# Keys and values in one ring of three 32 KB rows, and probabilities spread by 32 transposes a group, copied out by two engines

## The chip, the cores and the metric

The kernel runs on one NeuronCore of a Trainium2 chip. The metric is device time in microseconds (us) of one execution. The core has five engines that run their own instruction streams: TensorE (PE, matrix multiply, with its weight loads shown as PEld), VectorE (DVE), ScalarE (ACT), GpSimd (POOL) and SyncE (SP), which here only issues DMA transfers. Each stream is in order; an instruction waits on semaphores for what other engines or transfers must have finished. Everything behind a waiting instruction in the same stream waits too.

## What is computed

One decode step (one token, batch 1) of an attention block followed by a small MLP block. Cut to what matters here:

```python
# A: attention with a key/value cache; 32 query heads share 8 key/value heads, 4 to each
q = layernorm(x) @ wq                       # [1, 512] @ [512, 32*128]
scores = einsum("bhqd,bhkd->bhqk", q, k) * 128 ** -0.5     # k_cache [1, 8, 16384, 128] bf16
p = softmax(scores)
o = einsum("bhqk,bhkd->bhqd", p, v)         # v_cache [1, 8, 16384, 128] bf16
h = x + o.reshape(1, 1, 32 * 128) @ wo      # wo [4096, 512]
# B: with one token the shifted mixer gives zero, so hs @ w2 adds nothing; what is left is
y = layernorm(h)
out = h + y + gelu(layernorm(y) @ w3) @ w4  # w3 [512, 1792], w4 [1792, 512]
```

The bytes are almost all cache: 8 heads of keys and 8 of values, 4 MB (4,194,304 bytes) each, 67 MB in all. With wq and wo (4 MB each) and w3 and w4 (1.8 MB each) it is 79.2 MB.

## The kernel before

**Groups.** One key/value head with its four query heads is a group g, 0 to 7. A head's 16384 tokens lie as 128 partitions of 128 consecutive tokens, so one load of keys is 128 rows of 32 KB, one row to a partition.

**Buffers.** Keys have two buffers of 32 KB a partition (`kb`, L200). Values come in two halves of 8192 tokens, each 128 rows of 16 KB, into three buffers of 16 KB a partition (`vb`, L202); the two halves of the last group go into `kb[0]`. Together 112 KB a partition. The weights w3 and w4 go into `kb[1]` at the end.

**One round** of the loop at L461, for g from 0 to 8, does the scores of group g and the value sums of group g-1:

- DVE transposes the keys in 32x32 blocks, eight instructions a group (L379), from `kb` into `kt`. After the fourth of them the first half of the scores can be finished, after the eighth the second half.
- PE makes the scores in two halves of 16 matmuls each (L388) in `s_ps`: 128 partitions (column tile, query head) by 512 tokens a half.
- DVE takes the maximum of each half (L396); two small PE steps with DVE steps between them (L401 to L410) make one bias per head.
- ACT takes the exponential of each half (L414) into `p_sb`, 128 by 1024, and POOL copies its first 64 columns behind its end (L420).
- `weights(g)` (L422) brings the probabilities to the layout that the value sums need, tokens on partitions. PE transposes 16 windows of 128 columns, each 64 columns further than the last (L424), into the PSUM tile `T_ps`, which fills two banks, windows 0 to 7 and 8 to 15. DVE copies what is wanted out of them into `pt` with five copies of 64 partitions (L430).
- `denominator(g)` (L435) adds up the exponentials with two small matmuls.
- `values(g-1, A, qs)` (L444) multiplies `pt` of the group before with the value half A, 16 matmuls a half, into `O_ps`. In the order of PE the 16 of half A=0 stand between the two halves of the scores, the 16 of A=1 in two eights around the small steps of the maximum.
- `gather(g-1)` (L453, L456): DVE copies `O_ps` to `o_sb`, and PE adds it into `A_ps` with eight matmuls in fp32. In PE's order it stands behind `weights(g)`, and in DVE's order behind the copies of L430.

Round 8 has only values(7) and gather(7). Behind it come the division by the denominators, the product with wo (128 matmuls, L522), the second block's layernorm (a chain of small DVE instructions, L254 to L295), the products with w3 (L535) and w4 (L555) and the output.

**The queue of loads.** All loads of the loop are issued by SP at the end of each round, in order: x4 (by ACT), wq, k0, k1, then values of g (two halves) and keys of g+2 for each g, and after those of g=7 wo in three pieces, w3 in two, w4 in two. Each issue waits until the buffer that it fills has been read: a key load until the eight transposes of the group two before are done, a value load until the value matmuls of the buffer's last user are done.

**Order by hand.** `Program.op` (L35) works out the waits from the keys that an operation reads and writes, and from the PSUM banks it uses (an operation waits for the last one of every other engine on its bank). Operations of one engine keep the order in which they are written.

Of the kernel before, what the change touches and what calls it, by code (L numbers as in the profile page):

```python
# [112 lines left out]
HKV = 8  # L113
SK = 16384
DH = 128
# [8 lines left out]
KRING = 2  # L124
VRING = 3
VT = 64 * DH
# [4 lines left out]
def bass_sequential_preLN__gqa_block_cached__mixer_s_mlp__decode_kernel(  # L131
# [13 lines left out]
    with ExitStack() as ctx:  # L145
# [3 lines left out]

# [33 lines left out]
        p_sb = sb("p_sb", [128, 1024 + 64], BF16)  # L183
        pt = [sb(f"pt{i}", [128, 4, 2, 16, REP], BF16) for i in range(2)]
# [15 lines left out]
        kb = [sb(f"kb{i}", [128, 128 * DH], BF16) for i in range(KRING)]  # L200
        kt = sb("kt", [128, 128 * DH], BF16)
        vb = [sb(f"vb{i}", [128, VT], BF16) for i in range(VRING)]  # L202
        w3_sb = kb[1][:, 0:NCH * FM].rearrange("p (k f) -> p k f", k=NCH)
        w4_sb = kb[1][:, NCH * FM:2 * NCH * FM].rearrange("p (m c) -> p m c", m=NHC)
# [12 lines left out]
        def load_k(g):  # L217
            i = g % KRING
            load(f"k{i}", kb[i][:, :], A_k_cache[0, g].rearrange("(p t) d -> p (t d)", p=128), ("k", i, 0),
                 also=[("k", i, n) for n in range(1, 4)])  # L220

        def value_tile(g, A):

            if g == HKV - 1:
                return kb[0][:, A * VT:(A + 1) * VT], ("k", 0, A)
            i = (2 * g + A) % VRING
            return vb[i][:, :], ("v", i)

        def load_v(g, A):
            src = A_v_cache[0, g, A * 8192:(A + 1) * 8192, :].rearrange("(p t) d -> p (t d)", p=128)  # L230
            dst, key = value_tile(g, A)
            load("v" + "_".join(map(str, key[1:])), dst, src, key)
# [69 lines left out]
        load_k(0)  # L302
        load_k(1)
# [70 lines left out]
        def transpose_keys(g, ts):  # L374
            i = g % KRING
            for t in ts:
                view = lambda x, t=t: x[:, :].bitcast(I32).rearrange("p (x l w) -> p x (l w)", x=2, l=64)[
                    :, :, t * 512:(t + 1) * 512]
                dve(lambda e, i=i, view=view: e.transpose(view(kt), view(kb[i])),  # L379
                    r=[("k", i, n) for n in range(4)], w=[("kt", t)])  # L380

        ktv = kt[:, :].rearrange("p (x l b s e) -> p b e l x s", x=2, l=64, b=2, s=32, e=2)

        def scores(g, half):
            for n in range(4):
                for ct in range(4):
# [4 lines left out]
                        ktv[:, n // 2, n % 2, 8 * c8:8 * c8 + 8, :, :],  # L391
# [15 lines left out]
        def max_c(g):  # L407
# [5 lines left out]
            for half in range(2):  # L413
                act(lambda e, half=half, g=g: e.activation(  # L414
                    p_sb[:, half * 512:half * 512 + 512].rearrange("p (l s x) -> p l x s", l=8, x=2),
                    s_ps[:, half, :].rearrange("p (l x s) -> p l x s", l=8, x=2),
                    ACTF.Exp, bias=bias[:, 0:1], scale=float(SCALE), accum_out=acc[g % 2][:, half:half + 1]),
                    r=[("s", half), "bias"], w=[("p", half), ("acc", g % 2)], bank=[("s", half)])
                if half == 0:
                    P.op("POOL", lambda e: e.tensor_copy(p_sb[:, 1024:1088], p_sb[:, 0:64]), r=[("p", 0)], w=[("p", 2)])  # L420

        def weights(g):  # L422
            for w in range(16):
                pe(lambda e, w=w: e.transpose(T_ps[:, w, :], p_sb[:, w * 64:w * 64 + 128], ident[:, :]),  # L424
                   r=[("p", w // 8), ("p", (w + 1) // 8), "ident"], w=[("T", w // 8)], bank=[("T", w // 8)])
            to = pt[g % 2][:, :, :, :, :].rearrange("p c A l h -> p l (c A) h")
            of = T_ps[:, :, :].rearrange("p w (k o u h) -> p w k o u h", o=2, u=2, h=REP)
            for half, lo, w0, w1, l0 in ((0, 0, 0, 8, 0), (0, 64, 0, 8, 1), (1, 0, 8, 16, 8), (1, 64, 8, 15, 9),
                                         (1, 64, 15, 16, 0)):
                dve(lambda e, lo=lo, w0=w0, w1=w1, l0=l0: e.tensor_copy(  # L430
                    to[lo:lo + 64, l0:l0 + w1 - w0, :, :], of[lo:lo + 64, w0:w1, :, lo // 64, 0, :]),
                    r=[("T", half)], w=[("pt", g % 2)], bank=[("T", half)])
# [6 lines left out]
        def values(g, A, qs):  # L439
            tile, key = value_tile(g, A)  # L440
            for q in qs:
                for ct in range(4):
                    n = 32 * (q // 2) + 8 * ct + 4 * (q % 2)
                    pe(lambda e, q=q, ct=ct, n=n: e.matmul(  # L444
                        O_ps[g % 2][32 * ct:32 * ct + 16, :],
                        pt[g % 2][:, ct, A, 4 * q:4 * q + 4, :].rearrange("p l h -> p (l h)"),
                        tile[:, n * DH:(n + 4) * DH],
                        start=(A == 0 and q == 0), stop=(A == 1 and q == 3)),
                       r=[key, ("pt", g % 2)], w=[("O", g % 2)], bank=[("O", g % 2)])
# [11 lines left out]
        for g in range(HKV + 1):  # L461
# [6 lines left out]
            if g:  # L468
                values(g - 1, 0, range(4))
# [5 lines left out]
            if g:  # L475
                values(g - 1, 1, range(2))
            if g < HKV:
                max_b()
            if g:
                values(g - 1, 1, range(2, 4))  # L480
# [9 lines left out]
            if g < HKV:  # L490
                for A in range(2):
                    load_v(g, A)
                if g + 2 < HKV:
                    load_k(g + 2)
            if g == HKV - 1:
# [4 lines left out]
                for n, (lo, hi) in enumerate(W3):  # L500
                    load(f"w3{n}", w3_sb[:, lo:hi, :], w3_in[:, lo:hi, :], ("k", 1, n))
                w4_in = B_w4.rearrange("(p m) c -> p m c", p=128)
                for n, (lo, hi) in enumerate(W4):
                    load(f"w4{n}", w4_sb[:, lo:hi, :], w4_in[:, lo:hi, :], ("k", 1, 2 + n))
# [90 lines left out]
```

## Time and profile before

| | |
|---|---|
| median of 3 runs | 194.05 us (194.0 to 194.56) |
| the profiled execution | 194.11 us, of which the span from first to last instruction is 192.3 us |
| busy over the span | PE 112.5 us (58%), DVE 122.0 us (63%), ACT 16.9 us (9%), POOL 3.3 us (2%) |
| moved by DMA | 79.32 MB, mean 412 GB/s over the span |
| key transposes (L379) | 64 in 74.0 us, mean 1212 ns |
| transposes of probabilities (L424) | 128 in 11.7 us, mean 249 ns each while they overlap |
| copies out of them (L430) | 40 in 9.8 us |
| exponentials (L414) | 16, mean 822 ns |
| granted TensorE clock | mean 0.761 of full; in each part either 1.0 or 0.5 |

Lines of the profile name the source line, the engine, the operation, output and input tiles, and shapes. In a timeline row the first number is the start in us from the begin of the span, the second the length of the merged stretch; `x7` is the number of instructions in it, and the bracket is the time that the engine sat idle before it, with what ended that idle time. SPq is SP's instruction stream, in which a DMA row is the issue of a transfer, not the transfer.

### The profile page before, as it was taken

To read this page: it belongs to the slowest core of one execution; us is meant where nothing else is said; L and a number is where in the kernel's file an instruction comes from. 1 tells how busy PE (TensorE), PEld (TensorE's weight loads), DVE (VectorE), ACT (ScalarE), POOL (GpSimd) and SP (SyncE) were. 2 spreads that over 40 slices of the span, in tenths; PEclk is the share of its full clock that TensorE was granted. 3 is DMA by queue.
4 is the path that set the end of the run, shared out by engine and by line. 5 is a ranking of instruction groups with operands and counts; after the bars stand their busy time and mean duration, and the time that the engine had idled before them with its cause. 6 is when DMAs were issued, how large, how long until landed. Compare 5 with 4: busy or idle time off the path is not lost.

```text
span 192.3 us, 2624 instructions
## 1 busy us (share of the span) xinstructions
PE 112.5 (58%) x1106; PEld 56.3 (29%) x1106; DVE 122.0 (63%) x236; ACT 16.9 (9%) x38; POOL 3.3 (2%) x17
## 2 busy tenths in 40 slices
PE   1025046567837766774776558645885676594533
PEld 1025001242234235223422522242223422453402
DVE  5834099499449928964894379536944796403274
ACT  3000000030030030003000200030003000600010
POOL 2000000000000000000000000000000000000000
PEclk9999999999985695588559655975558559669555
DMA  6999999999999999999999999999999999999990
GB/s 225 429 436 433 436 436 426 423 455 436 395 429 467 436 388 429 460 423 409 426 436 436 419 423 436 443 426 416 450 441 399 416 429 436 417 421 424 421 376 34
DMA packets 4634, 79.32 MB, mean 412 GB/s; under 512 B 528, under 2 KB 528, under 8 KB 912
## 3 DMA queue, kind: packets, MB, share of 16 engines
q1 hardware_dynamic: 4616, 79.17, 96.8%
q8 instruction: 8, 0.13, 0.3%
q14 instruction: 2, 0.02, 0.0%
q10 hardware_dynamic: 8, 0.00, 0.0%
HBM read 79.17 MB, written 0.00 MB: 412 GB/s over the span
## 4 chain that ended last, share of the span: by engine, by line
DMA 47%; DVE 18%; issue 2%; PE 2%; SPq 1%; ACT 0%; DVEq 0%; ACTq 0%
DMA kb<-in_A_k_cache_dram 28%; DMA wqo<-in_A_wo_dram 19%; DVE kt L379 13%; PE O_ps L522 1%; DVE mx L396 1%; DVE st L293 1%; SPq L215 1%; DVE hcol L546 1%; DVE sti L295 0%; PE T_ps L424 0%; DVE pt L430 0%; PE mn_ps L260 0%; ACT hg L542 0%; DVE xs L550 0%; DVE st L295 0%
## 5 line engine op out<-in xcount | busy, mean ns | idle before, releaser
L379 DVE STREAM_TRANSPOSE kt<-kb 128x1024 int32<-128x1024 int32 x64 | 74.0, 1212 | 11.1 <-DMA kb<-in_A_k_cache_dram 11.0
L388 PE MATMUL s_ps<-kt,qb 128*32 128x512 bf16 x256 | 47.7, 557 | 32.0 <-DVE kt L379 32.0
L444 PE MATMUL O_ps<-vb,pt 128*16 128x512 bf16 x224 | 29.2, 533 | 0.0
L388 PEld LDWEIGHTS s_ps<-kt,qb 128*32 128x32 bf16 x256 | 10.7, 114 | 61.6 <-DVE kt L379 53.9
L414 ACT ACTIVATE p_sb<-s_ps,bias 128x512 bf16<-128x512 f32 x16 | 12.7, 822 | 149.9 <-PE mn_ps L408 113.8
L456 PE MATMUL A_ps<-o_sb,zo 128*128 128x128 f32 x64 | 15.7, 422 | 10.5 <-DVE o_sb L453 10.5
L430 DVE COPY pt<-T_ps 64x256 bf16<-64x256 bf16 (+2 forms) x40 | 9.8, 261 | 15.5 <-PE T_ps L424 15.2
L396 DVE TENSOR_REDUCE mx<-s_ps 128x1 f32<-128x512 f32 x16 | 10.8, 677 | 11.9 <-PE s_ps L388 9.8
L424 PE MATMUL T_ps<-ident,p_sb 128*128 128x128 bf16 x128 | 11.7, 249 | 11.0 <-ACT p_sb L414 11.0
L456 PEld LDWEIGHTS A_ps<-o_sb,zo 128*128 128x128 f32 x64 | 13.4, 311 | 11.6 <-DVE o_sb L453 11.6
L424 PEld LDWEIGHTS T_ps<-ident,p_sb 128*128 128x128 bf16 x128 | 8.8, 111 | 12.9 <-ACT p_sb L414 12.7
L444 PEld LDWEIGHTS O_ps<-vb,pt 128*16 128x16 bf16 x224 | 9.4, 115 | 10.0 <-issue 8.5
L357 PE MATMUL mn_ps<-xn,wqo 128*128 128x1 bf16 x128 | 3.6, 165 | 9.4 <-DMA wqo<-in_A_wq_dram 9.4
L401 PE MATMUL mn_ps<-ident_f,mx 128*1 128x128 f32 x32 | 7.3, 322 | 2.5 <-DVE mx L396 2.5
L453 DVE COPY o_sb<-O_ps 128x512 f32<-128x512 f32 x8 | 5.5, 692 | 5.0 <-PE O_ps L444 4.7
L357 PEld LDWEIGHTS mn_ps<-xn,wqo 128*128 128x128 bf16 x128 | 3.5, 104 | 9.4 <-issue 9.4
L404 DVE TENSOR_REDUCE nm<-mn_ps 1x4 f32<-1x256 f32 x8 | 3.3, 406 | 3.7 <-PE mn_ps L401 3.7
L522 PE MATMUL O_ps<-wqo,o_b 128*32 128x128 bf16 x128 | 3.1, 271 | 2.9 <-DMA wqo<-in_A_wo_dram 1.6
L420 POOL COPY p_sb<-p_sb 128x64 bf16<-128x64 bf16 x8 | 1.9, 237 | 160.5 <-ACT p_sb L414 160.5
L401 PEld LDWEIGHTS mn_ps<-ident_f,mx 128*1 128x1 f32 x32 | 2.3, 90 | 7.5 <-DVE mx L396 5.3
L408 PEld LDWEIGHTS mn_ps<-nm,nscale 1*128 1x128 f32 x16 | 2.5, 198 | 5.5 <-DVE nm L404 5.5
L408 PE MATMUL mn_ps<-nm,nscale 1*128 1x4 f32 x16 | 3.2, 270 | 1.2 <-DVE nm L404 0.9
(75 smaller groups left out, 51.7 us busy)
## 6 DMA issues: line engine op xcount, KB each, us to landing
kb<-in_A_k_cache_dram SPq DMA_DIRECT2D x8, 4096.0 KB, 26.3
vb<-in_A_v_cache_dram SPq DMA_DIRECT2D x14, 2048.0 KB, 24.2
wqo<-in_A_wq_dram SPq DMA_DIRECT2D x1, 4096.0 KB, 12.3
kb<-in_A_v_cache_dram SPq DMA_DIRECT2D x2, 2048.0 KB, 26.8
wqo<-in_A_wo_dram SPq DMA_DIRECT2D x2, 1792.0 KB, 34.7
kb<-in_B_w_dram SPq DMA_DIRECT2D x1, 1344.0 KB, 22.9
kb<-in_B_w_dram SPq DMA_DIRECT2D x1, 1280.0 KB, 26.2
wqo<-in_A_wo_dram SPq DMA_DIRECT2D x1, 512.0 KB, 37.4
```

What stands on the lines that cost most here:

```text
L357: pe(lambda e, h=h, k=k: e.matmul(n_ps[:, h:h + 1], wqo[:, k * HQ * DH + h * DH:k * HQ * DH + (h + 1) * DH], xn[:, k:k + 1], start=(k == 0 ...
L379: dve(lambda e, i=i, view=view: e.transpose(view(kt), view(kb[i])), r=[("k", i, n) for n in range(4)], w=[("kt", t)])
L388: pe(lambda e, g=g, half=half, n=n, ct=ct, c8=c8: e.matmul(s_ps[32 * ct:32 * ct + 32, half, :], qb[:, n, g, :, :, :].rearrange("p a u h -> ...
L396: dve(lambda e: e.tensor_reduce(mx[:, half:half + 1], s_ps[:, half, :], AX.X, ALU.max), r=[("s", half)], w=[("mx", half)], bank=[("s", half)])
L401: pe(lambda e, half=half: e.matmul(m_ps[0:1, half * 128:half * 128 + 128], mx[:, half:half + 1], ident_f[:, :], start=True, stop=True), r= ...
L408: pe(lambda e: e.matmul(n_ps[:, 0:REP], nscale[0:1, :], nm[0:1, :], start=True, stop=True), r=["nm", "nscale"], w=["n"], bank=["mn"])
L414: act(lambda e, half=half, g=g: e.activation(p_sb[:, half * 512:half * 512 + 512].rearrange("p (l s x) -> p l x s", l=8, x=2), s_ps[:, hal ...
L424: pe(lambda e, w=w: e.transpose(T_ps[:, w, :], p_sb[:, w * 64:w * 64 + 128], ident[:, :]), r=[("p", w // 8), ("p", (w + 1) // 8), "ident"] ...
L430: dve(lambda e, lo=lo, w0=w0, w1=w1, l0=l0: e.tensor_copy(to[lo:lo + 64, l0:l0 + w1 - w0, :, :], of[lo:lo + 64, w0:w1, :, lo // 64, 0, :]) ...
L444: pe(lambda e, q=q, ct=ct, n=n: e.matmul(O_ps[g % 2][32 * ct:32 * ct + 16, :], pt[g % 2][:, ct, A, 4 * q:4 * q + 4, :].rearrange("p l h -> ...
L453: dve(lambda e, g=g: e.tensor_copy(o_sb[g % 2][:, :], O_ps[g % 2][:, :]), r=[("O", g % 2)], w=[("osb", g % 2)], bank=[("O", g % 2)])
L456: pe(lambda e, g=g, j=j: e.matmul(A_ps[:, 0:128], zo[:, j, 112 - 16 * g:240 - 16 * g], o_sb[g % 2][:, j * 128:(j + 1) * 128], start=False, ...
```

## The change

Keys and values share one ring of three buffers of 32 KB a partition (`rb`, 96 KB a partition in all). The items go round it in the order of their loads: k0, k1, v0, k2, v1, k3, v2, and so on, item n into buffer n mod 3 (`ORDER`, `SLOT`). A group's values are loaded whole, 128 rows of 32 KB, by one transfer instead of two. So the tokens that one partition holds are 128 consecutive ones for values as for keys; the value matmuls of a group all wait for the one load. w3 and w4 go into buffer 16 mod 3 = 1, which k7 had.

Keys and values having the same layout, the exponential writes `p_sb` in the order in which it reads the scores (the order within the scores changes instead, in `ktv`), and the probabilities have to be spread differently. `weights(g)` now makes 32 transposes, each 32 columns further, in four sets of eight that take the two banks of `T_ps` in turn. Each set is copied out by four or more copies of 32 partitions: sets 0 and 2 by DVE with four copies each (8 a group), sets 1 and 3 by ACT with four and seven (11 a group; a window that would run over the end of the group's 32 columns is cut in two). POOL copies 96 columns instead of 64. The 32 value matmuls of a group are the same in number and shape; the first 16 stand in the same place in PE's order, the others too.

The diff, cut to its core (the renaming of `kb` to `rb` in the transposes and of the keys of w3 and w4 is left out):

```diff
-KRING = 2
-VRING = 3
-VT = 64 * DH
+RING = 3
+ORDER = [("k", 0), ("k", 1)] + [x for g in range(HKV) for x in (("v", g), ("k", g + 2)) if x[1] < HKV]
+SLOT = {x: n % RING for n, x in enumerate(ORDER)}
+FB = len(ORDER) % RING
+RPARTS = 4
...
-        p_sb = sb("p_sb", [128, 1024 + 64], BF16)
-        pt = [sb(f"pt{i}", [128, 4, 2, 16, REP], BF16) for i in range(2)]
+        p_sb = sb("p_sb", [128, 1024 + 96], BF16)
+        pt = [sb(f"pt{i}", [128, 4, 32, REP], BF16) for i in range(2)]
...
-        kb = [sb(f"kb{i}", [128, 128 * DH], BF16) for i in range(KRING)]
+        rb = [sb(f"rb{i}", [128, 128 * DH], BF16) for i in range(RING)]
...
-        vb = [sb(f"vb{i}", [128, VT], BF16) for i in range(VRING)]
...
-        def load_k(g):
-            i = g % KRING
-            load(f"k{i}", kb[i][:, :], A_k_cache[0, g].rearrange("(p t) d -> p (t d)", p=128), ("k", i, 0),
-                 also=[("k", i, n) for n in range(1, 4)])
-
-        def value_tile(g, A):
-
-            if g == HKV - 1:
-                return kb[0][:, A * VT:(A + 1) * VT], ("k", 0, A)
-            i = (2 * g + A) % VRING
-            return vb[i][:, :], ("v", i)
-
-        def load_v(g, A):
-            src = A_v_cache[0, g, A * 8192:(A + 1) * 8192, :].rearrange("(p t) d -> p (t d)", p=128)
-            dst, key = value_tile(g, A)
-            load("v" + "_".join(map(str, key[1:])), dst, src, key)
+        def load_tokens(kind, g):
+
+            i, src = SLOT[kind, g], A_k_cache if kind == "k" else A_v_cache
+            load(f"r{i}", rb[i][:, :], src[0, g].rearrange("(p t) d -> p (t d)", p=128), ("r", i, 0),
+                 also=[("r", i, n) for n in range(1, RPARTS)])
...
-        ktv = kt[:, :].rearrange("p (x l b s e) -> p b e l x s", x=2, l=64, b=2, s=32, e=2)
...
+        ktv = kt[:, :].rearrange("p (x l b s e) -> p b e x l s", x=2, l=64, b=2, s=32, e=2)
...
-                    p_sb[:, half * 512:half * 512 + 512].rearrange("p (l s x) -> p l x s", l=8, x=2),
-                    s_ps[:, half, :].rearrange("p (l x s) -> p l x s", l=8, x=2),
+                    p_sb[:, half * 512:half * 512 + 512], s_ps[:, half, :],
...
-                    P.op("POOL", lambda e: e.tensor_copy(p_sb[:, 1024:1088], p_sb[:, 0:64]), r=[("p", 0)], w=[("p", 2)])
+                    P.op("POOL", lambda e: e.tensor_copy(p_sb[:, 1024:1120], p_sb[:, 0:96]), r=[("p", 0)], w=[("p", 2)])
...
-            for w in range(16):
-                pe(lambda e, w=w: e.transpose(T_ps[:, w, :], p_sb[:, w * 64:w * 64 + 128], ident[:, :]),
-                   r=[("p", w // 8), ("p", (w + 1) // 8), "ident"], w=[("T", w // 8)], bank=[("T", w // 8)])
-            to = pt[g % 2][:, :, :, :, :].rearrange("p c A l h -> p l (c A) h")
-            of = T_ps[:, :, :].rearrange("p w (k o u h) -> p w k o u h", o=2, u=2, h=REP)
-            for half, lo, w0, w1, l0 in ((0, 0, 0, 8, 0), (0, 64, 0, 8, 1), (1, 0, 8, 16, 8), (1, 64, 8, 15, 9),
-                                         (1, 64, 15, 16, 0)):
-                dve(lambda e, lo=lo, w0=w0, w1=w1, l0=l0: e.tensor_copy(
-                    to[lo:lo + 64, l0:l0 + w1 - w0, :, :], of[lo:lo + 64, w0:w1, :, lo // 64, 0, :]),
-                    r=[("T", half)], w=[("pt", g % 2)], bank=[("T", half)])
+
+            of = T_ps[:, :, :].rearrange("p w (c a u h) -> p c w a u h", c=4, a=4, u=2)
+            for f in range(4):
+                b = f % 2
+                for w in range(8 * f, 8 * f + 8):
+                    pe(lambda e, w=w: e.transpose(T_ps[:, w % 16, :], p_sb[:, w * 32:w * 32 + 128], ident[:, :]),
+                       r=[("p", w // 16), ("p", (w + 3) // 16), "ident"], w=[("T", b)], bank=[("T", b)])
+                for a in range(4):
+                    n = 8 * f + a
+                    for lo, hi in ((n, min(n + 8, 32)), (32, n + 8)):
+                        if lo >= hi:
+                            continue
+                        args = (pt[g % 2][32 * a:32 * a + 32, :, lo % 32:lo % 32 + hi - lo, :],
+                                of[32 * a:32 * a + 32, :, 8 * b + lo - n:8 * b + hi - n, a, 0, :])
+                        if b == 0:
+                            dve(lambda e, args=args: e.tensor_copy(*args),
+                                r=[("T", b)], w=[("pt", g % 2, 0)], bank=[("T", b)])
+                        else:
+                            act(lambda e, args=args: e.copy(*args),
+                                r=[("T", b)], w=[("pt", g % 2, 1)], bank=[("T", b)])
...
-        def values(g, A, qs):
-            tile, key = value_tile(g, A)
+        def values(g, qs):
+            i = SLOT["v", g]
...
-                    n = 32 * (q // 2) + 8 * ct + 4 * (q % 2)
-                    pe(lambda e, q=q, ct=ct, n=n: e.matmul(
+                    half, x, l = q // 4, q // 2 % 2, 4 * (q % 2)
+                    t = 64 * x + 32 * half + 8 * ct + l
+                    pe(lambda e, q=q, ct=ct, t=t: e.matmul(
                         O_ps[g % 2][32 * ct:32 * ct + 16, :],
-                        pt[g % 2][:, ct, A, 4 * q:4 * q + 4, :].rearrange("p l h -> p (l h)"),
-                        tile[:, n * DH:(n + 4) * DH],
-                        start=(A == 0 and q == 0), stop=(A == 1 and q == 3)),
-                       r=[key, ("pt", g % 2)], w=[("O", g % 2)], bank=[("O", g % 2)])
+                        pt[g % 2][:, ct, 4 * q:4 * q + 4, :].rearrange("p l h -> p (l h)"),
+                        rb[i][:, t * DH:(t + 4) * DH], start=(q == 0), stop=(q == 7)),
+                       r=[("r", i, 0), ("pt", g % 2, 0), ("pt", g % 2, 1)], w=[("O", g % 2)], bank=[("O", g % 2)])
...
-                values(g - 1, 0, range(4))
+                values(g - 1, range(4))
...
-                values(g - 1, 1, range(2))
+                values(g - 1, range(4, 6))
...
-                values(g - 1, 1, range(2, 4))
+                values(g - 1, range(6, 8))
...
-                for A in range(2):
-                    load_v(g, A)
+                load_tokens("v", g)
                 if g + 2 < HKV:
-                    load_k(g + 2)
+                    load_tokens("k", g + 2)
```

## The prediction

> **What bounds the kernel now.** I read the slices of the page first, then windows of the length of two loads, then the chain of waits, then the timeline of the last two rounds.
>
> ```profile
> DMA  6999999999999999999999999999999999999990
> ...
> 24.00:43.50 19.50, 10.77 (x59) 4.35 (x59) 16.54 (x22) 1.64 (x4) 0.24 (x1) 1.00 1.00 431
> 111.80:131.30 19.50, 12.21 (x97) 5.55 (x96) 12.93 (x20) 1.64 (x4) 0.24 (x1) 0.68 1.01 429
> ```
>
> Columns of the windows: length, busy time of PE, PEld, DVE, ACT, POOL, granted clock, DMA share, GB/s. The DMA engines never rest, and the two 4 MB loads of a group take 19.5 us, whatever the engines do. DVE, the busiest, has 12.9 to 16.5 us of work in such a stretch. So the loads set the pace until the weights of the tail.
>
> ```profile
> 142.41 36.67 DMA wqo<-in_A_wo_dram
> 179.08 0.04 issue
> 179.13 2.14 PE O_ps L522 x70
> 181.26 0.02 issue
> 181.29 0.31 DVE hr L254 x2
> ```
>
> The chain that ended last runs through the second piece of wo, which lands at 179.1, the wo product, and from 181.29 a chain of small DVE steps to the end, 11.0 us long in the span of 192.3. The compute of the last groups is not on it. The question is how far it is from it:
>
> ```profile
> 150.93 6.88 DVE L379 STREAM_TRANSPOSE kt<-kb 128x1024 int32<-128x1024 int32 x6 [1.37 <-DMA kb<-in_A_k_cache_dram]
> 156.88 1.96 PE L444 MATMUL O_ps<-vb,pt 128*16 128x512 bf16 x16
> 160.72 1.10 PE L388 MATMUL s_ps<-kt,qb 128*32 128x512 bf16 x13 [0.74 <-DVE kt L379]
> 161.86 0.69 DVE L396 TENSOR_REDUCE mx<-s_ps 128x1 f32<-128x512 f32 x1 [1.20 <-PE s_ps L388]
> 164.16 0.82 ACT L414 ACTIVATE p_sb<-s_ps,bias 128x512 bf16<-128x512 f32 x1 [16.93 <-PE mn_ps L408]
> 165.08 1.91 PE L424 MATMUL T_ps<-ident,p_sb 128*128 128x128 bf16 x16 [1.21 <-ACT p_sb L414]
> 167.03 0.67 DVE L430 COPY pt<-T_ps 64x256 bf16<-64x256 bf16 x3 [0.26 <-PE T_ps L424]
> 168.47 2.07 PE L456 MATMUL A_ps<-o_sb,zo 128*128 128x128 f32 x8 [1.16 <-DVE o_sb L453]
> 170.47 2.62 PE L444 MATMUL O_ps<-kb,pt 128*16 128x512 bf16 x32
> 176.51 0.96 PE L522 MATMUL O_ps<-wqo,o_b 128*32 128x128 bf16 x56 [1.30 <-DVE o_b L516]
> 179.13 2.11 PE L522 MATMUL O_ps<-wqo,o_b 128*32 128x128 bf16 x72 [1.65 <-DMA wqo<-in_A_wo_dram]
> ```
>
> Round 7 starts when k7 lands (150.9). Its first exponential, which I call E, starts at 164.16; values(7) start at 170.47 = E + 6.31, behind gather(6); wo can start at 176.51, 6.04 later; at 177.5 PE has used the first piece and waits 1.65 us for the second. That wait is all the slack that the compute has at the end: about 1.65 us.
>
> **The change part by part.**
>
> Longer rows for values. The packet records of the trace have 16 KB packets at 0.616 us and 32 KB packets at 1.228 us. A value load is 8 rows of 32 KB to each of 16 DMA engines: 16 x 0.616 = 9.86 us against 8 x 1.228 = 9.82. Over 8 groups that is 0.3 us, with 8 fewer transfers to signal (9 ns each). Bounds: the DMA share of 1.00 to 1.01 in the windows leaves no gap to win; I keep 0 to 0.5, and take 0.3 sooner for every landing of the tail.
>
> A ring with less room, 96 KB for 112. It costs nothing as long as each load is issued before the one ahead of it ends; then the transfer in front hides it. The issues of SP show when buffers come free:
>
> ```profile
> 49.09 0.33 SPq L215 DMA_DIRECT2D kb<-in_A_k_cache_dram  x1
> ...
> 67.19 0.33 SPq L215 DMA_DIRECT2D kb<-in_A_k_cache_dram  x1
> ```
>
> At 49.09 the transposes of k1 are done, at 67.19 those of k2. In the new ring v1 takes k1's buffer and v2 takes k2's. k0 landed at 24.0, so k2 lands 3 x 9.76 later, at 53.3, and k3 at 72.8. With the rounds 1.2 and 2.2 us late (below) v1 is issued at 50.3, v2 at 69.4: 3.0 and 3.4 us before the queue runs dry, against 1.0 us from the first issue (0.74) to the first packet (1.78). Later buffers come free earlier against their load (k4's at 102.0, its turn at 111.8). Cost 0; without that cover each us adds a us.
>
> Values in one load. This is a new wait. Until now the first 16 value matmuls of a round needed half A, which lands 4.9 us before half B. Now they need all of v, and they stand on PE in front of the second half of the scores. In round 7 v6 lands at 150.9 + 9.8 - 0.3 = 160.4, 3.5 us after these matmuls began before (156.88). PE stands still till then, and behind it scores(7,1), the maximum, the bias and the exponentials. So: 160.45, then 16 value matmuls 1.96 (row of 156.88), 16 scores at half clock 1.89 (the row of the first half, 13 matmuls), then from the last scores to the exponential 164.16 - 161.82 = 2.34. E = 166.6, 2.5 later. Lower bound with the clock up: 1.31 (half of the 2.62 of 170.47), 1.10, 2.34: E = 165.2. Of 3.5 us, 1 is taken up by PE's old wait for the last key transposes (until 160.72).
>
> The same wait meets every round from 5 on, but there the loads hide it: from v5 (140.7) E of round 6 is 146.9, round 7's transposes begin 5 us later, 151.9, and 151.9 + 13.2 = 165.1, before 166.6.
>
> Spreading in 32 windows. Transposes: at full clock 0.65 us for eight, at half 0.95 (16 in 1.91). DVE copy of 32 partitions x 128 elements: no such row; the copies of L430 take 171 ns with 32 elements and 286 with 256, a line through both gives 220; upper bound 281 (L369, 32x128 from fp32). Four take 0.88. ACT copy: no row; an ACTIVATE of one element takes 202 ns, one of 224 takes 486, so 128 take 364 by the line; the exponentials begin 0.77 apart with 0.18 between them, so 0.13 overlaps. Four take 1.07 to 1.46, I use 1.25; the seven of the last set (512 elements in all) 1.28 to 2.06, I use 1.65.
>
> By the Trainium skill (ScalarE: Activation LUTs, What ACT_TABLE_LOAD costs) an ACTIVATE without pointer operands takes 186 ns + 0.833 ns an element and neighbours overlap by 93 ns; as an estimate from it the four take 0.89 and the seven 1.17 us. That is under my lower ends and would put `pt` 0.8 us sooner; the sum stays, since the gather ends later.
>
> The sets form a chain, in us after E, full / half clock: set 0 transposed 1.57 / 1.88, copied by DVE 2.49 / 2.80; set 1 transposed 2.05 / 2.84, copied by ACT 3.35 / 4.13; set 2 copied 4.09 / 4.72; set 3, which needs ACT's bank, transposed 4.03 / 5.13, copied 5.73 / 6.83. Behind set 2 on DVE stands the copy to `o_sb` (0.69), behind set 3 on PE the denominators (0.35 / 0.53) and gather(g-1) (1.16 / 2.07): it ends at 6.0 / 7.7, and then values may start. I take 7.0 against 6.31. DVE is held 0.9 to 1.2 us longer a group; in rounds 1 to 6 the loads hide it, since 17.1 us a round (transposes at 57.40 and 74.48) becomes 18.2, under 19.5.
>
> Layout of the scores and exponentials: same counts and shapes; 0, between -0.1 and +0.1 each. POOL's copy is 96 columns for 64, off the path.
>
> **The sum.** E 166.6 + 7.0 = 173.6 values(7); + 6.04 = 179.6 for wo; 128 matmuls at 17 (56 in 0.96) to 29 ns (72 in 2.11), 2.2 to 3.75, taken as 3.0: 182.6 where the chain had 181.29. All behind it follows, so the span is 192.3 + 1.35. Against the profiled execution (194.11) that is 195.45, against the median of 194.05 **195.4 us**. All at half clock: 166.6 + 7.7 + 8.0 + 3.75 = 186.05, +4.8.
>
> **The rivals.**
>
> *The slack takes it* (not slower). PE at full clock in round 7: E 165.2, + 6.0 + 6.04 = 177.2; plus 0.96 the first wo piece is used up by 178.2, before the second lands at 178.8. Then the landing still decides, and 0.3 comes off: 193.75. It decides while wo can start by 177.9. For it: the clock was up from 158 to 165 before. Against: PE will stand still from 159 to 160.4, and windows show it granted 0.5 where it pauses.
>
> *The ring runs dry.* If a round's weights cost 2.5 us more than counted, v1 is issued at 52.8 and v2 at 74.4, stalls of 0.5 and 2.1 more with the 1.0 us start: all landings 2.6 later, and of the 2.5 itself a part again behind the last exponentials: 195.4 + 2.6 + 1 = 199. It decides from 2 us a round. Against: copies are short; for: at 49.09 the old buffers had loads queued up to 63.0, and the new ring only up to 53.3.
>
> *Fewer transfers* (faster). If a gap lay between two loads, up to 2% of 9.8 us by the windows' shares, 8 fewer would give 8 x 0.2 = 1.6: 192.4. By the Trainium skill (DMA: Bandwidth & Descriptors, Anatomy of one DMA) each transfer has a fixed 2.0 us beside its bytes; it says so of the other kind of queue, and loads that follow each other at 429 GB/s show none of it.
>
> **How the numbers follow.** Forecast 0.60, slack 0.22, dry ring 0.11, fewer transfers 0.04, others 0.03. A measurement here tells 0.3%, 0.6 us, from no change. Faster: the fewer transfers and the low end of the slack, 0.08. Same: the rest of the slack and the low end of the forecast, 0.22. Slower 0.70. Range 193.7 (slack) to 198.5 (half clock); the forecast alone 194.4 to 198.5.
>
> **What would show it.** PE idle before L444's first matmuls in rounds 5 to 7, ended by the value load; E of round 7 near 166.6; values(7) near 173.6; no wait, or a short one, of L522 for wo; no slice of DMA under 9. It is wrong if the DMA row has holes, if set 3 on ACT and not the gather holds values(7), or if L522 still waits 1 us for wo.

## The result, and the profile after

| | before | after |
|---|---|---|
| median | 194.29 us (6 runs, 194.0 to 194.56) | 196.31 us (6 runs, 195.92 to 197.86) |
| ratio | 1 | 1.0122, 95% interval 1.0097 to 1.0147 |
| profiled execution, span | 194.11 us, 192.3 us | 197.86 us, 196.1 us |

The kernel is slower by 2.0 us. The profiled execution of after is its longest: four of its six runs took 195.92 to 196.38 us, the other two 197.61 and 197.86. So what follows is about where things start, and the experiments decide on medians.

First the slices of after, the rows of the DMA engines. Each column is 1/40 of the span, 4.9 us.

```profile
DMA  6999999999899999999999999999999999999940
GB/s 221 461 435 445 428 441 448 428 430 428 324 428 428 428 411 428 428 435 431 423 428 428 431 428 435 436 435 424 428 448 435 424 428 428 398 424 411 418 174 0
```

Before, no slice but the first and the last was under 9. Now slice 11 has 8 and 324 GB/s: once, near 51 us, most of the loading stopped. The windows put a size on it (columns as in the prediction: length, busy time of PE, PEld, DVE, ACT, POOL, granted clock, DMA share, GB/s). First the stretch before, then the same stretch after and 2 us out of it:

```profile
43.50:63.00 19.50, 14.21 (x108) 6.29 (x112) 14.19 (x21) 1.63 (x4) 0.24 (x1) 0.82 1.01 429
```
```profile
43.50:63.00 19.50, 14.47 (x119) 7.98 (x117) 14.47 (x25) 4.85 (x22) 0.27 (x1) 0.82 0.98 409
50.50:52.50 2.00, 1.65 (x32) 0.74 (x25) 0.69 (x1) 0.00 (x0) 0.00 (x0) 1.00 0.89 262
```

20 GB/s less over 19.5 us is 0.39 MB, or 0.9 us of the full rate, lost as a mean of the 16 DMA engines. SP's issues stand beside it:

```profile
33.77 0.33 SPq L215 DMA_DIRECT2D rb<-in_A_k_cache_dram  x1
50.39 0.33 SPq L215 DMA_DIRECT2D rb<-in_A_v_cache_dram  x1
53.17 0.33 SPq L215 DMA_DIRECT2D rb<-in_A_k_cache_dram  x1
```

These are k2, v1 and k3. v1 is issued at 50.39, when only the rest of k2 is in front of it. The packet records of the trace show what that meant for the 16 DMA engines (k2's packets end with a small one that reports the engine's part as done). The records do not name the engine. But where one packet follows another at once, it starts within 8 ns of the other's end, and so the packets can be paired:

```
after            k2's last packet ends    v1's first packet starts    and takes
13 engines       50.94 to 51.38           51.35 to 52.24              1.30 to 2.22 us
 2 engines       52.51 to 52.52           52.51 (no gap)              1.21 to 1.26 us
 1 engine        52.28                    54.06                       2.07 us
```

Thirteen engines had nothing to do for 0.5 us in the mean, one for 1.8 us, and the first packets of these fourteen took up to 2.2 us in place of 1.23. Why one of them begins 3.7 us after the issue the records do not show. On 15 engines v1 is complete by 62.72, on the late one at 64.95, 11.96 behind k2 where every later load takes 9.7 to 10.7. Nothing behind it can make up for that: v6 lands at 163.14 (160.69 before, 160.4 in the prediction).

The end of the program, in the timeline of after:

```profile
163.18 1.88 PE L443 MATMUL O_ps<-rb,pt 128*16 128x512 bf16 x16 [2.08 <-DMA rb<-in_A_v_cache_dram]
...
164.85 1.92 PE L377 MATMUL s_ps<-kt,qb 128*32 128x512 bf16 x16
...
169.66 0.69 ACT L403 ACTIVATE p_sb<-s_ps,bias 128x512 bf16<-128x512 f32 x1 [14.87 <-PE mn_ps L397]
...
171.15 0.92 DVE L426 COPY pt<-T_ps 32x128 bf16<-32x128 bf16 x4 [1.57 <-PE T_ps L416]
171.59 1.06 ACT L429 COPY pt<-T_ps 32x128 bf16<-32x128 bf16 x4 [0.49 <-PE T_ps L416]
172.13 1.89 PE L416 MATMUL T_ps<-ident,p_sb 128*128 128x128 bf16 x16 [0.57 <-DVE pt L426]
...
174.05 1.22 ACT L429 COPY pt<-T_ps 32x128 bf16<-32x128 bf16 x7 [1.40 <-PE T_ps L416]
174.15 0.69 DVE L451 COPY o_sb<-O_ps 128x512 f32<-128x512 f32 x1
174.90 2.08 PE L454 MATMUL A_ps<-o_sb,zo 128*128 128x128 f32 x8 [0.56 <-DVE o_sb L451]
...
176.91 2.86 PE L443 MATMUL O_ps<-rb,pt 128*16 128x512 bf16 x32
...
183.19 1.97 PE L519 MATMUL O_ps<-wqo,o_b 128*32 128x128 bf16 x128 [1.30 <-DVE o_b L513]
185.21 0.29 DVE L243 TENSOR_SCALAR_CACHE_REDUCE hr<-O_ps 128x128 f32<-128x128 f32 x1 [2.08 <-PE O_ps L519]
```

PE waits for the load of v6 and from there on every step hangs on the one ahead of it: E is 169.66, values(7) 176.91, the wo product 183.19, hr 185.21. The product no longer waits for wo (its second piece landed at 181.48). Hence the chain that ended last is another, here before and after:

```profile
DMA 47%; DVE 18%; issue 2%; PE 2%; SPq 1%; ACT 0%; DVEq 0%; ACTq 0%
```
```profile
DVE 41%; DMA 30%; PE 20%; issue 4%; ACT 2%; SPq 0%; DVEq 0%; ACTq 0%
```

PE now has 20% of it, where before it had 2%. And two rows of groups, for the new copies and for the wait of the values (last columns: busy us, mean ns, idle before):

```profile
L426 DVE COPY pt<-T_ps 32x128 bf16<-32x128 bf16 x64 | 14.1, 220 | 19.5 <-PE T_ps L416 18.8
L443 PE MATMUL O_ps<-rb,pt 128*16 128x512 bf16 x256 | 29.7, 531 | 9.6 <-DMA rb<-in_A_v_cache_dram 9.6
```

### The profile page after: what moved, and what is told of

Same layout as the page of the kernel before. It is cut to its first block, busy times and chain, and to the rows that moved or that the text cites. A ratio compares the mean times of both kernels' runs of the same rounds, so it can differ in the third digit from the quotient of the medians.

```text
span 196.1 us, 2987 instructions
## 1 busy us (share of the span) xinstructions
PE 117.4 (60%) x1234; PEld 63.9 (33%) x1234; DVE 126.0 (64%) x260; ACT 33.1 (17%) x126; POOL 3.5 (2%) x17
## 4 chain that ended last, share of the span: by engine, by line
DVE 41%; DMA 30%; PE 20%; issue 4%; ACT 2%; SPq 0%; DVEq 0%; ACTq 0%
DVE kt L368 27%; DMA rb<-in_A_v_cache_dram 19%; DMA rb<-in_A_k_cache_dram 12%; PE O_ps L443 6%; DVE pt L426 5%; PE T_ps L416 5%; PE s_ps L377 4%; DVE mx L385 3%; ACT p_sb L403 2%; PE A_ps L454 2%; PE mn_ps L397 1%; PE mn_ps L390 1%; DVE o_sb L451 1%; PE O_ps L519 1%; DVE st L282 1%
## 5 line engine op out<-in xcount | busy, mean ns | idle before, releaser
L368 DVE STREAM_TRANSPOSE kt<-rb 128x1024 int32<-128x1024 int32 x64 | 74.0, 1212 | 4.6 <-DMA rb<-in_A_k_cache_dram 4.6
L377 PE MATMUL s_ps<-kt,qb 128*32 128x512 bf16 x256 | 41.6, 552 | 25.1 <-DVE kt L368 25.1
L443 PE MATMUL O_ps<-rb,pt 128*16 128x512 bf16 x256 | 29.7, 531 | 9.6 <-DMA rb<-in_A_v_cache_dram 9.6
L416 PE MATMUL T_ps<-ident,p_sb 128*128 128x128 bf16 x256 | 22.7, 254 | 12.9 <-ACT p_sb L403 9.0
L377 PEld LDWEIGHTS s_ps<-kt,qb 128*32 128x32 bf16 x256 | 10.4, 117 | 50.3 <-DVE kt L368 40.8
L426 DVE COPY pt<-T_ps 32x128 bf16<-32x128 bf16 x64 | 14.1, 220 | 19.5 <-PE T_ps L416 18.8
L416 PEld LDWEIGHTS T_ps<-ident,p_sb 128*128 128x128 bf16 x256 | 18.6, 115 | 16.0 <-ACT p_sb L403 9.7
L429 ACT COPY pt<-T_ps 32x128 bf16<-32x128 bf16 (+6 forms) x88 | 17.7, 226 | 14.1 <-PE T_ps L416 13.5
L454 PE MATMUL A_ps<-o_sb,zo 128*128 128x128 f32 x64 | 13.4, 375 | 6.3 <-DVE o_sb L451 6.3
L443 PEld LDWEIGHTS O_ps<-rb,pt 128*16 128x16 bf16 x256 | 8.8, 107 | 22.3 <-DMA rb<-in_A_v_cache_dram 13.8
L408 POOL COPY p_sb<-p_sb 128x96 bf16<-128x96 bf16 x8 | 2.1, 266 | 165.7 <-ACT p_sb L403 165.7
```

The costliest lines, as they stand in the source:

```text
L368: dve(lambda e, i=i, view=view: e.transpose(view(kt), view(rb[i])), r=[("r", i, n) for n in range(RPARTS)], w=[("kt", t)])
L377: pe(lambda e, g=g, half=half, n=n, ct=ct, c8=c8: e.matmul(s_ps[32 * ct:32 * ct + 32, half, :], qb[:, n, g, :, :, :].rearrange("p a u h -> ...
L416: pe(lambda e, w=w: e.transpose(T_ps[:, w % 16, :], p_sb[:, w * 32:w * 32 + 128], ident[:, :]), r=[("p", w // 16), ("p", (w + 3) // 16), " ...
L426: dve(lambda e, args=args: e.tensor_copy(*args), r=[("T", b)], w=[("pt", g % 2, 0)], bank=[("T", b)])
L429: act(lambda e, args=args: e.copy(*args), r=[("T", b)], w=[("pt", g % 2, 1)], bank=[("T", b)])
L443: pe(lambda e, q=q, ct=ct, t=t: e.matmul(O_ps[g % 2][32 * ct:32 * ct + 16, :], pt[g % 2][:, ct, 4 * q:4 * q + 4, :].rearrange("p l h -> p ...
```

## The experiments

Three questions: Is the dry ring the cause, or the wait for whole values, or the spreading? Each set ran on one chip with the kernel before (194.2, 194.21 and 194.27 us in the three sets). Landings are those of the last DMA engine. Where a kernel has "one projection", a single matmul stands in place of the 128 of the query projection, so that all heads get the same query.

### The old buffers with the new spreading

```diff
-RING = 3
+KRING = 2
+VRING = 3
+VT = 64 * DH
...
-        rb = [sb(f"rb{i}", [128, 128 * DH], BF16) for i in range(RING)]
+        rb = [sb(f"rb{i}", [128, 128 * DH], BF16) for i in range(KRING)]
+        vb = [sb(f"vb{i}", [128, VT], BF16) for i in range(VRING)]
```

Values come in two halves of 16 KB rows again and each half has a wait of its own.

> The changed kernel with the buffers of before: two of 32 KB for keys, three of 16 KB for halves of the values (a half is now 64 of the 128 tokens of each partition), the first 16 value matmuls needing only the first half. Left of the change: the spreading by 32 transposes, the layout. Theory (ring and wait cost the time, the spreading hides): no hole in the DMA row, values(7) about 7.2 us after the last round's first exponential instead of 6.3, taken up by the 1.65 us wait for wo: 193.7 to 194.5 us. Rival (the spreading costs it): 195 us or more, with L519 not waiting for wo.

Measured: 195.7 us (195.28 to 198.0), ratio 1.0106 (1.0065 to 1.0147). The slices show no hole, v6's second half lands at 161.2, hr is at 182.22, but the time is only 0.6 us under that of after. In the profiled execution the last piece of w4 lands at 190.98 (before 189.01) and the end waits for its product. So without a dry ring a second loss shows up, in the loads of the tail.

### Values in two halves, ring kept

```diff
+                for x in range(2):
+                    load(f"r{i}v{x}", rb[i][:, x * 64 * DH:(x + 1) * 64 * DH], rows[:, x * 64 * DH:(x + 1) * 64 * DH],
+                         ("r", i, 2 * x), also=[("r", i, 2 * x + 1)])
...
-                       r=[("r", i, 0), ("pt", g % 2, 0), ("pt", g % 2, 1)],
+                       r=[("r", i, 2 * x), ("pt", g % 2, 0), ("pt", g % 2, 1)],
```

> The changed kernel, ring and spreading kept, but each group's values loaded in two halves of 16 KB rows, and the first 16 value matmuls need only the first. Theory: the hole of the DMA row at 51 us stays, the wait of the value matmuls in rounds 4 to 7 shrinks to under 1 us, the first exponential of round 7 comes 2 to 3 us earlier, and wo's landing (181.5) takes over: 194.5 to 195 us. Rival (the late loads alone cost the time): 196.0 to 196.5 us.

Measured: 196.43 us (195.63 to 197.14), ratio 1.0115 (1.0094 to 1.0136): no better than after. The hole is there (289 GB/s in the same slice; v1 is issued at 50.54). E does come at 167.70, 2.0 sooner than in after, but the loads are as late (v6 at 163.28, the last of w4 at 191.69), and now the w4 product ends last. The wait for whole values is not what makes after slow as long as the loads are late.

### v1 and v2 in two parts, the first issued sooner

```diff
+EARLY = (1, 2)
...
+            if kind == "v" and g in EARLY:
+                for n in range(2):
+                    load(f"r{i}e{n}", tile[:, :, n * 32 * DH:(n + 1) * 32 * DH], rows[:, :, n * 32 * DH:(n + 1) * 32 * DH],
+                         ("r", i, 2 * n), also=[("r", i, 2 * n + 1)])
```

The parts hold the tokens of key transposes 0 to 3 and 4 to 7, so the first part of v1 may be issued when four of the eight transposes of k1 are done. The value matmuls still wait for both parts.

> The changed kernel with the loads of v1 and v2 alone cut in two parts, the first issued when four of the eight key transposes are done instead of eight; the value matmuls still wait for both parts. Theory (the ring ran dry): no hole at 51 us, all landings behind it 1.1 to 2.2 us earlier, and the end with them: 194.2 to 195.3 us. Rival (the hole is made good later, or lies on engines that wait anyway): 196.0 to 196.5 us.

Measured: 195.44 us (195.03 to 196.18), ratio 1.0072 (1.0054 to 1.0089), 0.9 us under after. The first part is issued at 45.28, and the window in which after moved 409 GB/s has

```profile
43.50:63.00 19.50, 12.66 (x121) 6.30 (x118) 14.90 (x25) 4.85 (x22) 0.27 (x1) 1.00 1.02 429
```

v6 lands at 160.99, hr is at 181.91, and then the end waits for the w4 product, whose weights land at 190.41:

```profile
191.13 0.29 DVE L565 TENSOR_TENSOR fin<-xsum,mn_ps 128x128 bf16<-128x128 f32 x1 [0.82 <-PE mn_ps L561]
```

The dry ring is part of the loss. What is left ends as with the old buffers, on the last weights.

### Both: parts issued sooner, and values by halves

```diff
-                       r=[("r", i, 0), ("r", i, 2), ("pt", g % 2, 0), ("pt", g % 2, 1)],
+                       r=[("r", i, 2 * half if g in EARLY else 2 * x), ("pt", g % 2, 0), ("pt", g % 2, 1)],
```

The other groups' values are loaded in two halves as in the second experiment.

> Both edits of the two runs before: v1 and v2 in two early parts, the other values in halves, the first 16 value matmuls needing only the first part. Theory: neither hole nor wait; what is left is the spreading, hidden by the wait for wo: 193.6 to 194.3 us, no slower than the kernel before. Rival (the spreading costs): 195 us or more.

Measured: 195.86 us (195.73 to 198.13), ratio 1.0109 (1.0076 to 1.0143). E is at 166.22 and hr at 181.70, the last of w4 lands at 190.88 and decides. Not better than the third: with the loads in order the wait for whole values is not what is left.

### What delays the last loads?

The late piece in the tail is late on one DMA engine (with the old buffers w3's second piece is complete at 186.62 on the last engine and at 185.26 on the last but one). The records show one way in which an engine falls behind: beside the loads there is a queue of instructions, packets of 16 KB that take 0.9 to 1.1 us of one engine. Before has 8 of them, after 9 and the 128 more transposes bring 256 more PE instructions with their weight loads. So PE instructions were added to before and taken from after.

Before, with 128 matmuls of one column that nobody reads, in front of the projection:

```diff
+        for n in range(128):
+            pe(lambda e: e.matmul(mn_ps[:, 0:1], ident[:, :], ident[:, 0:1], start=True, stop=True),
```

> The kernel before, with 128 small matmuls more on PE in the first 13 us, where PE waits for wq; they compute nothing that is used. Theory (more PE instructions mean one more 16 KB transfer on the instruction queue, which puts one DMA engine behind and with it the end of the last loads): nine such transfers instead of eight, the last piece of w4 about 0.6 to 1.1 us later: 194.6 to 195.4 us. Rival (those transfers cost nothing): 194.0 to 194.5 us.

Measured: 195.31 us (195.01 to 195.36), ratio 1.005 (1.0037 to 1.0063): 1.1 us for matmuls that PE makes while it would wait for wq. The page has 9 instruction packets; k0 lands as before (23.92), w3's second piece at 186.09 (184.69 before), and the gelu waits for the w3 product, where before it waited for DVE's chain:

```profile
186.75 0.85 ACT L546 ACTIVATE hg<-s_ps,st 128x224 bf16<-128x224 f32 x2 [17.72 <-PE s_ps L539]
```

Before, with the first 16 value matmuls waiting for both halves (the wait alone, no other part of the change):

```diff
-                       r=[key, ("pt", g % 2)], w=[("O", g % 2)], bank=[("O", g % 2)])
+                       r=[value_tile(g, 0)[1], value_tile(g, 1)[1], ("pt", g % 2)], w=[("O", g % 2)], bank=[("O", g % 2)])
```

> The kernel before, with one wait more: the first 16 value matmuls of a round wait for both halves of the values. Theory (this wait is the term behind the last exponentials): PE stands still up to 160.7 in round 7, its first exponential starts near 167.0 instead of 164.2, values(7) near 173.3, wo near 179.4, and the end moves by 0.3 to 1.7: 194.5 to 195.9 us. Rival (the slack before wo takes it): 194.0 to 194.5 us.

Measured: 194.45 us, ratio 1.0033 (1.0 to 1.0066). The median hides two groups: 8 of 12 runs have 193.82 to 194.65 at a mean granted clock of 0.748 to 0.769, 4 have 196.15 to 196.69 at 0.735 to 0.743. The profiled execution is one of the four:

```profile
150.00:165.00 15.00, 10.10 (x69) 4.75 (x70) 11.49 (x16) 0.00 (x0) 0.00 (x0) 0.50 1.01 429
```
```profile
161.21 1.88 PE L444 MATMUL O_ps<-vb,pt 128*16 128x512 bf16 x16 [2.71 <-DMA vb<-in_A_v_cache_dram]
...
167.66 0.82 ACT L414 ACTIVATE p_sb<-s_ps,bias 128x512 bf16<-128x512 f32 x1 [18.26 <-PE mn_ps L408]
```

The granted clock in that window was 0.72 before and is 0.50 here; E is 3.5 later. So the wait is free in most runs and costs 2 us in the others. That the clock of round 7 decides which is argued from this one trace and the means; no run of the larger group has a trace.

After with one projection (254 PE instructions fewer), and the kernel of the third experiment with it:

```diff
-        for h in range(HQ):
-            for k in range(NCH):
-                pe(lambda e, h=h, k=k: e.matmul(n_ps[:, h:h + 1],
-                                                wqo[:, k * HQ * DH + h * DH:k * HQ * DH + (h + 1) * DH],
-                                                xn[:, k:k + 1], start=(k == 0), stop=(k == NCH - 1)),
+        pe(lambda e: e.matmul(n_ps[:, 0:HQ], wqo[:, 0:DH], copies(xn[:, 0:1], HQ), start=True, stop=True),
```

> The changed kernel, with the 128 matmuls of the query projection at the start replaced by one, so that all heads have the same query: 254 PE instructions fewer, at a time when PE waits anyway. Theory (instruction transfers): eight instead of nine, landings at the end 0.5 to 1.1 us earlier than in the changed kernel: 195.2 to 195.8 us. Rival: 196.0 to 196.5 us.

> The changed kernel with the early loads of v1 and v2, and with the query projection in one matmul as in the run before. Theory (instruction transfers delay the last loads, which end this kernel): w4 lands at 189.3 instead of 190.4, and the chain behind the wo product decides: 194.2 to 194.8 us. Rival: 195.2 to 195.7 us, as without the shorter projection.

Measured: 194.06 us (193.58 to 195.52), ratio 1.0001 (0.9981 to 1.0022), and 194.56 us (194.02 to 196.6), ratio 1.0029 (1.0007 to 1.0051). The first is 2.2 us under after, more than late loads in the tail can explain. The trace shows why. In after an instruction packet at 19.45 us hits the load of k0, which is complete at 23.78 on the last engine and at 22.63 on the last but one. With one projection there is none at that time, and k0 lands at 22.71. Everything up to v1's issue follows k0's landing (from 23.8 on DVE waits three times, 1.98, 0.68 and 1.13 us, each time for PE and not for a load), so v1 is issued at 49.32 in place of 50.39, and the window that had 262 GB/s has 426:

```profile
49.32 0.33 SPq L215 DMA_DIRECT2D rb<-in_A_v_cache_dram  x1
```
```profile
50.50:52.50 2.00, 1.50 (x19) 0.60 (x13) 1.06 (x3) 0.00 (x0) 0.00 (x0) 1.00 1.08 426
```

1.07 us sooner was enough for the ring not to run dry: v1 lands 9.73 behind k2, not 11.96. In the kernel of the third experiment the two parts of v1 then only cost: together they take 9.95 us against 9.73 for the whole, for v1 and v2 0.44 us, about the 0.5 between the two kernels.

### The test of this: delay alone, a shorter projection, the spreading alone

One more transpose of the first keys in round 0, into a tile that nobody reads, in the kernel with one projection. It moves v1's issue back and leaves the projection and the number of PE instructions alone:

```diff
+                if g == 0:
+                    dve(lambda e: e.transpose(view0(wqo), view0(rb[0])),
+                        r=[("r", 0, n) for n in range(RPARTS)], w=[("wo", n) for n in range(len(WO))])
                 transpose_keys(g, range(3 if g == 1 else 0, 4))
```

> The kernel after with one projection matmul (194.06) and one more key transpose in round 0 (1.21 us on DVE, its result is read by nobody), so that v1 is issued near 50.5, as in the kernel after, while the instruction transfers stay as they are with one projection. Theory (dry ring decides from about 3 us before the landing in front): v1 lands some 11.5 to 12 us behind k2, every later load 1.5 to 2.2 later, time 195.6 to 196.3. Rival (what the one projection won came from fewer instruction transfers at the end, not from the sooner issue of v1): 194.1 to 194.4.

Measured: 196.22 us (194.77 to 196.82), ratio 1.0092 (1.0065 to 1.0119). The issue of v1 and the GB/s of the slices:

```profile
50.49 0.33 SPq L215 DMA_DIRECT2D rb<-in_A_v_cache_dram  x1
```
```profile
GB/s 215 430 444 444 444 437 430 457 432 430 313 430 437 430 407 430 444 430 427 432 423 430 427 430 430 439 423 420 430 437 430 427 430 430 405 424 412 418 260 4
```

The hole is back in the same slice, v1 lands 11.49 behind k2, v6 at 163.04, and 1.17 us of delay cost 2.2 us of time (196.22 - 194.06; 1.8 by the two ratios). PE's code is the same as with one projection, so the number of instructions is not what made after slow; the moment of v1's issue is.

After with the query projection turned round: xn stationary, wq moving, 32 matmuls and 8 transposes in place of 128 matmuls:

```diff
+        for blk in range(8):
+            for k in range(NCH):
+                pe(lambda e, blk=blk, k=k: e.matmul(
+                    s_ps[32 * (blk % 4):32 * (blk % 4) + 32, blk // 4, :], copies(xn[:, k:k + 1], 32),
+                    wqo[:, k * HQ * DH + blk * 512:k * HQ * DH + (blk + 1) * 512],
...
+        for w in range(8):
+            pe(lambda e, w=w: e.transpose(T_ps[:, w, :], p_sb[:, w * 128:w * 128 + 128], ident[:, :]),
```

> The kernel after with the query projection turned round: xn is the stationary operand (32 copies of a column), wq moves in 512 columns, so 32 matmuls in place of 128, then two copies and eight transposes bring the queries to the same layout; 176 PE instructions fewer (with their weight loads), all of them before the first keys land. Theory (instruction transfer early on, then a dry ring): the transfer at 19.45 us, during the load of k0, is gone, k0 lands near 22.7 in place of 23.8, v1 is issued near 49.3, v1 lands 9.7 behind k2 in place of 12.0, and the time is near that with one projection matmul, 194.1 (193.7 to 194.7). Rival (only the leaving out of the projection's work mattered, or the number of instruction transfers is not what delays k0): k0 at 23.8 and 195.9 to 196.4.

Measured: 194.51 us (193.64 to 195.91), ratio 1.0021 (0.9996 to 1.0046): 1.8 of the 2.0 us are back in a kernel with ring, whole values and spreading as in after. k0 lands at 22.76, v1 is issued at 49.37 and lands 9.82 behind k2:

```profile
49.37 0.33 SPq L215 DMA_DIRECT2D rb<-in_A_v_cache_dram  x1
...
161.04 1.89 PE L452 MATMUL O_ps<-rb,pt 128*16 128x512 bf16 x16 [1.89 <-DMA rb<-in_A_v_cache_dram]
...
167.17 0.69 ACT L412 ACTIVATE p_sb<-s_ps,bias 128x512 bf16<-128x512 f32 x1 [14.32 <-PE mn_ps L406]
...
173.71 2.89 PE L452 MATMUL O_ps<-rb,pt 128*16 128x512 bf16 x32
...
180.02 1.97 PE L528 MATMUL O_ps<-wqo,o_b 128*32 128x128 bf16 x128 [1.30 <-DVE o_b L522]
182.04 0.29 DVE L243 TENSOR_SCALAR_CACHE_REDUCE hr<-O_ps 128x128 f32<-128x128 f32 x1 [2.08 <-PE O_ps L528]
```

The page of this kernel has 9 instruction packets, as many as after's; what changed is that the first comes at 42.97 and not during the load of k0 (and the last at 189.45, when the loads are all but over).

The same projection in before:

> The kernel before with the same turned projection: 176 PE instructions fewer. Theory: before, the late k0 costs nothing in the ring (its loads are issued 9 us ahead), but the last loads of the slowest DMA engine come up to 1.0 us sooner where no transfer hits it behind: 193.0 to 194.2, so at best faster than both kernels. Rival (instruction transfers do not move the end before, which is set by the wo landing of 179.1): 194.2 within 0.2.

Measured: 194.37 us (193.84 to 195.05), ratio 1.0006 (0.9995 to 1.0017). k0 lands at 22.69 here too, and it is worth nothing: with the old buffers the load behind k2 is issued at 33.05, long before k2 ends. No kernel of this study is faster than before beyond the noise.

The spreading alone, that is the old buffers of the first experiment with one projection:

> The spreading in 32 windows alone: old buffers (two for keys, three halves for values) and one projection matmul, so that the PE instructions are about as many as before. Theory (the spreading itself is hidden or costs under 0.5, its 256 PE instructions cost through their transfers): 194.1 to 194.7, against 195.7 with the whole projection. Rival (the longer chain from exponentials to values costs the time): 195.4 to 195.8.

Measured: 194.46 us (194.17 to 196.8), ratio 1.0017 (0.9996 to 1.0039). The 32 windows and the two copying engines cost 0.2 us in the median, 0.4% at the end of the interval. The first experiment, 1.2 us slower, has the same spreading and 254 PE instructions more; w3's second piece lands at 185.32 here and at 186.62 there. That the instruction packets make this difference is argued from the idle matmuls and not shown: both kernels have such a packet during w3 (at 183.46 here, at 183.78 there).

## Why the prediction was right and wrong

**The bound.** Right: loads without a pause up to the tail, and a compute chain 1.65 us behind them at the end. The prediction's own sign against it, holes in the DMA row, came up.

**The ring: the step that failed.** The prediction put it at "Cost 0", since v1 would be issued at 50.3, "3.0 and 3.4 us before the queue runs dry" for v1 and v2. The issue was sized rightly (50.39). The moment at which the queue runs dry was not: the prediction took the landing of k2, 53.3. That is when the last engine has reported. On 13 of the 16 engines k2's last packet had ended by 50.94 to 51.38, 1.6 to 2.0 us before the landing of 52.99. And where the prediction put 1.0 us from issue to first packet, 13 engines took 1.0 to 1.9 and one took 3.7. Counted so, the fastest engine needed the issue of v1 by about 49.1 to 50.0: no slack was left, but a lack of 0.4 to 1.3. The runs bracket it: issues at 49.32 and 49.37 cost nothing, issues at 50.39 and 50.49 let v1 land 2.2 and 1.8 us late. These 2 us are what the sum did not have. The rival in which the ring runs dry had the right mechanism, but began it 2.5 us too late and made it hit v2 as well; only v1 was hit, as v2's issue (68.71) came 2.7 us before the first engine's last packet of k3 (71.44).

**Longer rows.** Foreseen 0.3 sooner for every landing of the tail. With the ring in order v6 lands at 160.51 and 160.99 against 160.69 before; with the turned projection in both it is 160.99 against 160.93. A gain of 0.3 is not seen. The term was mis-sized: the 0.616 us of a 16 KB packet is a mean that holds the eight instruction packets at 1.06. The loads' own take 0.6146, so that 16 of them make 9.83 against 9.82, under 0.1 us over 8 groups.

**Values in one load.** The mechanism was right: PE waits for v6, and E comes 6.2 behind its landing in the sum, 6.5 in after, 6.2 with the turned projection, 5.7 with one projection. That it can be free, as the rival of the slack said, is shown by the wait put into before: 193.8 to 194.65 in most runs, 2 us more in the others. That this takes the full clock, as the rival had it, is not shown. The runs of the turned projection split too, 7 of 193.64 to 194.70 and 5 of 195.23 to 195.91, but there the mean granted clock does not tell the two groups apart (0.731 to 0.823 against 0.736 to 0.771), and why they split stays open. With the old buffers and one projection, where each half has its own wait, 11 of 12 lie within 194.17 to 194.60.

**The spreading.** The copies were sized well: DVE 220 ns as forecast, four ACT copies 1.06 and seven 1.22 us against 1.25 and 1.65. By the Trainium skill (ScalarE: Activation LUTs, What ACT_TABLE_LOAD costs) the estimate had been 0.89 and 1.17: the trace lies between, nearer to the page for the seven. From E to values(7) 7.0 were forecast; after has 7.25, the turned projection 6.54, one projection 5.92. The gather ends last there, as the prediction said.

**The product with wo.** Taken as 3.0, it takes 1.97 in after (at a granted clock of 1.00) and with the turned projection, and 3.36 with one projection (at 0.56). So with the ring in order hr comes at 182.04 and 180.89, not 182.6: the terms other than the ring were too large by 0.6 to 1.7 us. The forecast of 195.4 was nearer to 196.31 than its sum deserved, by luck: with the ring in order the runs give 194.06 (one projection) and 194.51 (turned projection).

**What was not in the sum at all.** The transfers of instructions. The prediction counted instructions by their time on the engine and not by their code. In after it is not their number that decides (the delayed kernel has eight of them, as many as before, and is as slow as after), but where one falls: at 19.45 on the load of k0. It was there before, too (18.43, k0 at 23.98), where nothing hung on it.

## What to carry to other kernels

Where a buffer's next load is issued, count its lead up to the last packet of the load in front on the fastest DMA engine, not up to that load's landing. Here an issue 1.5 or 1.6 us before that packet's end (3.8 and 4.1 before the landing) cost nothing, one 0.6 or 0.5 us before it (2.6 and 2.9 before the landing) cost 2 us. Here the lead was short only at the start, for v1, before the ring had settled; that is the place to look at. The loss was not made up in the 100 us of loads behind it. A change that adds instructions can add transfers of code: look where they fall among the loads, and shift work (here a projection with fewer instructions) so that they fall where a load has time.

## What was not expected of the hardware

- In after the engines that ran dry lost time twice: 0.5 us in the mean without a packet (one engine 1.8 us; in the kernel with the late keys, too, one engine begins only at 53.85), and 1.30 to 2.22 us for the first packet of 32 KB in place of 1.23. The second loss does not need a dry engine: with one projection eleven first packets of v1, which follow without a gap, take 1.34 to 1.69.
- The 16 KB packets of instructions (8 or 9 in a run) take 0.9 to 1.1 us of one DMA engine, and that engine is as late in the next load: in after the last engine ends k0 1.15 us behind the last but one, and k1 1.13 behind it. Before with 128 idle matmuls has one packet more, its w4 lands 1.25 us later, and it takes 1.1 us longer.
- The engines that share a load drift apart: in after the last one reports a load 1.6 us behind the first at 51 us, and 3.7 us behind it from k6 on (134.00 against 130.31).
- The same wait of PE costs nothing or 2 us in one and the same kernel; the mean granted clock of the run goes with it (0.748 to 0.769 against 0.735 to 0.743).
